# Fetching the first expert's last 128 rows two steps later: attention, a dense layer and eight experts on one core

## The chip, the cores and the metric

The kernel runs on 1 core of one Trainium2 chip. The metric is the device time of one execution in microseconds (us), from the first to the last instruction and what the launch puts around them. TensorE is called PE here, VectorE DVE, ScalarE ACT, GpSimd POOL; SP is the queue that issues most transfers.

## The reference

Three parts follow each other. The first is an attention over 4 batches, 8 heads, 576 positions and 64 features: a coarse one over means of 4 positions plus a local one in a band of 7. Its output is laid out as 2304 tokens of 512 features. The second is a dense layer, the third a mixture of experts in which each token goes to one of 8 experts:

```python
h = x @ w_in; x = (h * np.cos(h)) @ w_out
logits = x @ w_gate
expert_idx = np.argmax(logits, axis=1)
...
for e in range(E):
    mask = expert_idx == e
    xe = x[mask]
    ye = np.maximum(xe @ w1[e], 0.0) @ w2[e]
    out[mask] = gate_w[mask, None] * ye
```

## The kernel before

Products are made in float32 precision: each operand is split into a high part and a rest, and three matmuls (high by high, high by rest, rest by high) are summed. The dense layer runs over 9 blocks of 256 tokens and 8 pairs of hidden chunks (`hidden`, `project`); the attention of the later batches is woven into it. After each block `route` finds each token's expert and scatters its number into lists in DRAM (`lists`), one list per expert and parity.

Before the last block, `freeze` picks the expert with most tokens so far. It is the first expert to run (e = 0 below), and its first 256 rows are known then; its last 128 rows (window 2) and the order of the others are known only when the last block is routed. So the first expert runs in two parts. The loop over f = 0 to 7 in `run` computes windows 0 and 1: `expert_hidden` makes hidden chunk f + 2 (tiles `eph`, then `hh` on ACT and `hl` on DVE) and `expert_project` adds chunk f to the two sums `eacc`. Then `expert_late` makes the hidden layer of window 2 in one piece (`eph_late`, `late`, `latet`), and a second loop projects it.

`expert_fetch` brings an expert's rows. SP loads two rows of token numbers (`listed`), DVE takes the smaller of each pair (L602), PE transposes the result (`ids_ps`, L605), DVE makes indices of it (`esrc`, `ids`, L607 and L609), and POOL gathers the rows (`rows`, L613). `expert_rows` then turns each 128 rows on PE (`ext`, L631), ACT copies them as the high part (`exh`, L633) and DVE subtracts for the rest (`exl`, L634). `expert_chunk` loads a chunk of the next expert's two weights (`raw`, two transfers of 512 KB, L574) and splits each into high part and rest, two casts on ACT (L579) and two subtractions on DVE (L580) for each; `put` scales a sum (`y`, L704) and scatters it to the output.

In the loop over f the calls stand so: at f = 2 the fetch of window 2, at f = 4 the fetch of the next expert's three windows (e = 1), at f = 5 `expert_rows` of window 2, and at odd f one chunk (0 to 3) of the next expert's weights. A block `issue_after` ties the transposition of token numbers on PE behind the last matmul written before it (`self.lastmm`).

The order in which the instructions stand on each engine is not the order of the code. A scheduler decides it when the program is built, from its own estimate of when each operand is ready; on the chip each engine then works through its list in that order and waits where an operand is missing.

Of the kernel before, what the change touches and what calls it, by code (L numbers as in the profile page):

```python
# [32 lines left out]
class Kernel:  # L33
# [556 lines left out]
        nc.vector.reciprocal(gt, sm)  # L590
        return gt

    def expert_fetch(self, e, w0, nw, last, behind=None):

        nc, NT = self.nc, self.NT
        n_ = f"{e}_{w0}"
        listed = self.stage.tile([nw, 3, P], I32, tag="w32", bufs=self.W32, name=f"listed{n_}")
        for t in range(2):
            src = self.lists[t][bass.ds(self.number[e] * NT + w0 * P, nw * P), :]
            nc.sync.dma_start(out=listed[:, t, :], in_=src.rearrange("(w p) c -> w (p c)", p=P))  # L600
        idf = listed[:, 2, :].bitcast(F32)
        nc.vector.tensor_tensor(out=idf, in0=listed[:, 0, :], in1=listed[:, 1, :], op=ALU.min)  # L602
        ps = self.psum([P, nw], f"ids_ps{n_}")
        with self.tc.issue_after(behind) if behind else nullcontext():
            nc.tensor.transpose(ps, idf, self.ident[:nw, :nw])  # L605
        src = self.ep.tile([P, self.NW], I32, tag="esrc", bufs=3, name=f"esrc{n_}")
        nc.vector.tensor_scalar(out=src[:, :nw], in0=ps, scalar1=float(last), scalar2=None, op0=ALU.min)  # L607
        ids = self.ep.tile([P, self.NW], I32, tag="ids", bufs=4, name=f"ids{n_}")
        nc.vector.tensor_copy(ids[:, :nw], ps)  # L609
        got = []  # L610
        for w in range(nw):
            rows = self.ep.tile([P, self.RW], F32, tag="rows", bufs=3, name=f"rows{e}_{w0 + w}")
            nc.gpsimd.indirect_dma_start(out=rows, out_offset=None, in_=self.rows[:last + 1, :],  # L613
                                         in_offset=bass.IndirectOffsetOnAxis(ap=src[:, w:w + 1], axis=0))
            got.append((w0 + w, ids[:, w:w + 1], rows))
        return got
# [144 lines left out]
    def run(self):  # L761
        nc, tc, E, NT, KD = self.nc, self.tc, self.E, self.NT, self.KD
# [171 lines left out]
        for s, (i, fp) in enumerate(slots):  # L934
# [35 lines left out]
            if (i, fp) == (self.NB - 2, 6):  # L970
                assert next(routing, 0) == 0
                self.number = self.freeze()
                got = self.expert_fetch(0, 0, 2, i * self.TB - 1)
# [13 lines left out]
        for f in range(self.NFE):  # L987
            if f + 2 < self.NFE:
                hs.append(self.expert_hidden(0, f + 2, xs, 2 * P))
            if f == 1:  # L990
                gates = self.expert_gates(0, got)
                number, over = self.rest()
                self.number += number
            if f == 2:
                got = self.expert_fetch(0, 2, 1, NT - 1, self.lastmm)
            if f == 5:
                self.expert_rows(0, got, xs)
            if f == 4:
                nxt = self.expert_fetch(1, 0, self.windows(1), NT - 1, self.lastmm)
            if f % 2 == 1:  # L1000
                self.expert_chunk(1, f // 2)
            self.expert_project(0, f, hs[f], ((0, 0), (1, 1)))
# [11 lines left out]
        for e in range(1, E):  # L1014
            gates = self.expert_gates(e, nxt)
            cols, nw = CAPS[e], self.windows(e)
            last = e == E - 1
# [70 lines left out]
```

## Time and profile before

| what | value |
|---|---|
| median of 3 runs | 875.44 us (874.58 to 875.65) |
| the profiled execution's own time | 877.69 us |
| its span, first to last instruction | 875.9 us |
| mean granted clock of PE | 0.979 |
| PE busy | 830.3 us, 95% of the span |
| DVE busy / ACT busy / POOL busy | 61% / 57% / 23% |
| moved by DMA | 95.87 MB, mean 109 GB/s |

The profile is one execution; its own time is 2.25 us above the median. In a timeline a row gives start, length, engine, line, operation, the tile written and the tiles read, how often, and in brackets the idle time of the engine just before with what ended it. The granted clock is a share: 1.00 stands for 2.4 GHz and 0.50 for 1.2 GHz.

### The profile page before, as it was taken

How to read it: one execution, taken by the hardware profiler on the slowest of the kernel's cores; microseconds unless marked ns; L12 is line 12 of the kernel's file. 1: busy time of each engine (PE TensorE's matmuls, PEld its weight loads, DVE VectorE, ACT ScalarE, POOL GpSimd, SP SyncE). 2: the span in 40 equal slices, each digit the busy share in tenths (PEclk: the TensorE clock that was granted, in tenths of full speed). 3: DMA queues.
4: the chain of work that ended last, by engine and by line, in shares of the span. 5: the costliest groups of instructions: out<-in, count | busy, mean ns of one | idle time of the engine just before them, and what ended most of it. 6: DMA issues, size and time to landing. Idle time of an engine off the chain costs nothing.

```text
span 875.9 us, 16801 instructions
## 1 busy us (share of the span) xinstructions
PE 830.3 (95%) x6130; PEld 711.9 (81%) x6130; DVE 537.7 (61%) x1293; ACT 495.4 (57%) x1246; POOL 197.6 (23%) x356
## 2 busy tenths in 40 slices
PE   6889799999999999999999999999899999999995
PEld 4667578778788888788898888898788888888895
DVE  5885799876444485476666657586447654555320
ACT  5466766676766875675644444583366544544321
POOL 5252344442222212313101010100121112012200
PEclk9989899999999999999999999999899999999998
DMA  9931783233252024022010101241748746446110
GB/s 202 290 79 38 295 247 96 71 82 85 59 167 64 14 76 105 13 73 73 15 49 1 49 1 49 73 123 47 192 143 292 243 135 212 148 160 198 58 38 22
DMA packets 112695, 95.87 MB, mean 109 GB/s; under 512 B 65120, under 2 KB 92844, under 8 KB 112604
## 3 DMA queue, kind: packets, MB, share of 16 engines
q1 hardware_dynamic: 108492, 83.96, 32.8%
q0 software_dynamic: 4112, 10.76, 4.1%
q8 instruction: 50, 0.82, 0.4%
q14 instruction: 41, 0.34, 0.1%
HBM read 81.31 MB, written 13.98 MB: 109 GB/s over the span
## 4 chain that ended last, share of the span: by engine, by line
PE 59%; DMA 6%; issue 5%; ACT 5%; DVE 5%; POOL 2%; POOLq 0%; DVEq 0%; ACTq 0%
PE acc L423 16%; PE h L395 15%; PE eacc L671 10%; PE eph L652 9%; DMA lists<-tokens,posi 2%; ACT p L203 1%; DMA raw<-in_moe_w_dram 1%; DMA out_dram<-y,ids 1%; PE o L261 1%; DVE prod L471 1%; PE o L250 1%; PE ext L631 1%; DMA rows<-rows,esrc 1%; PE ptd L238 1%; PE eph_late L689 1%
## 5 line engine op out<-in xcount | busy, mean ns | idle before, releaser
L395 PE MATMUL h<-xh,w 128*128 128x256 f32 x1152 | 230.0, 289 | 0.6 <-ACT xh L322 0.5
L423 PE MATMUL acc<-w,gh 128*128 128x512 f32 x576 | 191.5, 408 | 10.9 <-issue 4.5
L395 PEld LDWEIGHTS h<-xh,w 128*128 128x128 f32 x1152 | 185.8, 192 | 5.5 <-DVE w L366 0.9
L395 PE MATMUL h<-xl,w 128*128 128x256 f32 x576 | 165.4, 287 | 1.4 <-DVE xl L323 1.4
L423 PEld LDWEIGHTS acc<-w,gh 128*128 128x128 f32 x576 | 103.4, 190 | 30.6 <-issue 4.7
L423 PE MATMUL acc<-w,gl 128*128 128x512 f32 x288 | 117.6, 408 | 1.8 <-DVE gl L409 1.8
L652 PE MATMUL eph<-exh,w 128*128 128x256 f32 (+5 forms) x512 | 118.1, 307 | 0.0
L395 PEld LDWEIGHTS h<-xl,w 128*128 128x128 f32 x576 | 110.5, 192 | 4.2 <-DVE xl L323 1.6
L580 DVE TENSOR_TENSOR w<-raw,w 128x512 fp32r<-128x512 f32 x128 | 83.3, 687 | 32.5 <-ACT w L579 32.2
L671 PE MATMUL eacc<-w,hh 128*128 128x512 f32 (+4 forms) x304 | 99.2, 407 | 0.3 <-ACT hh L660 0.3
L652 PEld LDWEIGHTS eph<-exh,w 128*128 128x128 f32 x512 | 87.9, 190 | 3.3
L579 ACT CAST w<-raw 128x512 fp32r<-128x512 f32 x128 | 73.6, 618 | 29.3 <-DMA raw<-in_moe_w_dram 16.3
L401 ACT ACTIVATE u<-h 128x512 int32<-128x512 f32 x72 | 43.2, 600 | 79.7 <-PE h L395 79.6
L652 PE MATMUL eph<-exl,w 128*128 128x256 f32 (+5 forms) x256 | 78.7, 307 | 0.0
L405 DVE SCALAR_TENSOR_TENSOR u<-u,h 128x512 f32<-128x512 f32 x72 | 49.3, 684 | 47.6 <-ACT u L404 47.2
L402 DVE SCALAR_TENSOR_TENSOR u<-h,u 128x512 f32<-128x512 f32 x72 | 49.4, 686 | 38.5 <-ACT u L401 36.3
L471 DVE SCALAR_TENSOR_TENSOR prod<-row,wgb 128x512 f32<-128x512 f32 x96 | 67.1, 699 | 7.4 <-ACT row L465 6.0
L423 PEld LDWEIGHTS acc<-w,gl 128*128 128x128 f32 x288 | 54.5, 189 | 14.4 <-DVE gl L409 2.5
L408 ACT CAST gh<-u 128x512 fp32r<-128x512 f32 x72 | 44.6, 619 | 35.8 <-DVE u L405 21.3
L499 POOL DMA_INDIRECT lists<-tokens,posi x18 | 19.0, 1057 | 198.2 <-DVE posi L496 192.3
L403 ACT ACTIVATE u<-u 128x512 f32<-128x512 f32 x72 | 45.5, 632 | 31.8 <-DVE u L402 30.8
L671 PEld LDWEIGHTS eacc<-w,hh 128*128 128x128 f32 (+4 forms) x304 | 52.1, 182 | 12.0 <-ACT hh L660 0.8
(177 smaller groups left out, 1416.3 us busy)
## 6 DMA issues: line engine op xcount, KB each, us to landing
raw<-in_moe_w_dram SPq DMA_DIRECT2D x64, 512.0 KB
f<-in_moe_w_in_dram SPq DMA_DIRECT2D x8, 1024.0 KB
f<-in_moe_w_out_dram SPq DMA_DIRECT2D x8, 1024.0 KB
rows<-row SPq DMA_DIRECT2D x9, 520.0 KB
xraw<-xT SPq DMA_DIRECT2D x14, 256.0 KB
rawk<-in_k_dram SPq DMA_DIRECT2D x48, 72.0 KB
rawv<-in_v_dram SPq DMA_DIRECT2D x24, 144.0 KB
rawq<-in_q_dram SPq DMA_DIRECT2D x32, 80.0 KB
```

The costliest lines, as they stand in the source:

```text
L395: nc.tensor.matmul(ph[:, fo, :], lhsT=a[:, kk, f], rhs=b[:, kk, :], start=(n == 0), stop=(n == 3 * self.KD - 1))
L401: nc.scalar.activation(turns, hv, AF.Copy, scale=1.0 / (2 * math.pi))
L402: nc.vector.scalar_tensor_tensor(out=u, in0=hv, scalar=1.0 / (2 * math.pi), in1=turns, op0=ALU.mult, op1=ALU.subtract)
L403: nc.scalar.activation(u, u, AF.Sin, scale=PI)
L405: nc.vector.scalar_tensor_tensor(out=u, in0=u, scalar=1.0, in1=hv, op0=ALU.subtract, op1=ALU.mult, reverse0=True)
L408: nc.scalar.copy(gh, u)
L423: nc.tensor.matmul(self.acc[i][t], lhsT=a[:, fo, t * P:(t + 1) * P], rhs=b[:, fo, :], start=(f == 0 and n == 0), stop=(f == self.NF - 1 an ...
L471: nc.vector.scalar_tensor_tensor(out=prod, in0=row[:, t, :DM], scalar=1.0, in1=self.spread[e // 2][:, e % 2, :], op0=ALU.mult, op1=ALU.mul ...
L579: nc.scalar.copy(hi, raw[:, sl])
L580: nc.vector.tensor_tensor(out=lo, in0=raw[:, sl], in1=hi.bitcast(F32), op=ALU.subtract)
L652: self.lastmm = nc.tensor.matmul(ph, lhsT=a[:, kk, f % 2 * P:(f % 2 + 1) * P], rhs=b[:, kk, :cols], start=(n == 0), stop=(n == 3 * self.KD ...
L671: self.lastmm = nc.tensor.matmul(self.eacc[w][:m], lhsT=a[:, at * P:at * P + m], rhs=b[:, f % 2, :], start=(f == 0 and n == 0), stop=(f == ...
```

## The change

`expert_fetch` is cut in two. `expert_list` holds its first half (the two transfers of token numbers and the minimum on DVE) and is still called at f = 2 for window 2; the second half (transposition, indices, gather) now follows at f = 4. The turning of window 2's rows goes from f = 5 to f = 7, and the whole fetch of the next expert from f = 4 to f = 6.

```diff
-    def expert_fetch(self, e, w0, nw, last, behind=None):
+    def expert_list(self, e, w0, nw):
...
         idf = listed[:, 2, :].bitcast(F32)
         nc.vector.tensor_tensor(out=idf, in0=listed[:, 0, :], in1=listed[:, 1, :], op=ALU.min)
+        return idf
+
+    def expert_fetch(self, e, w0, nw, last, behind=None, idf=None):
+
+        nc = self.nc
+        n_ = f"{e}_{w0}"
+        if idf is None:
+            idf = self.expert_list(e, w0, nw)
         ps = self.psum([P, nw], f"ids_ps{n_}")
...
             if f == 2:
-                got = self.expert_fetch(0, 2, 1, NT - 1, self.lastmm)
-            if f == 5:
+                idf = self.expert_list(0, 2, 1)
+            if f == 4:
+                got = self.expert_fetch(0, 2, 1, NT - 1, self.lastmm, idf)
+            if f == 7:
                 self.expert_rows(0, got, xs)
-            if f == 4:
+            if f == 6:
                 nxt = self.expert_fetch(1, 0, self.windows(1), NT - 1, self.lastmm)
```

The lists below show what the scheduler makes of both. In a name the first number is the step f (of `eph`, `hh`, `hl`), the window (of `ids_ps`, `ext`, `rows`, `y`, `eacc`) or the chunk (of `raw`), the last a serial number; lines of the changed kernel are 8 higher.

On PE, the transposition of window 2's token numbers (`ids_ps_2`) in the loop of the first expert, before:

```order
L671 MATMUL eacc_1_7813<-w_1_7544,hl_4_7986 128x512
L652 MATMUL eph_7_8083<-exh_7389,w_0_7602 128x256
L605 MATMUL ids_ps_2_7993<-ident,listed_2_7989 128x1
L652 MATMUL eph_7_8083<-exl_7390,w_0_7602 128x256
L652 MATMUL eph_7_8083<-exh_7389,w_0_7602 128x256 x2
```

and now:

```order
L679 MATMUL eacc_1_7813<-w_1_7544,hl_4_7986 128x512
L660 MATMUL eph_7_8067<-exh_7389,w_0_7602 128x256
L613 MATMUL ids_ps_2_8053<-ident,listed_2_7989 128x1
L660 MATMUL eph_7_8067<-exl_7390,w_0_7602 128x256
L660 MATMUL eph_7_8067<-exh_7389,w_0_7602 128x256 x2
```

It stands between the same two matmuls as before. Nothing ahead of it on PE has moved either.

On PE, the end of that loop and the start of `expert_late`, before (`ids_ps_0` is the next expert's transposition, `ext_2` the turning of window 2's rows):

```order
L671 MATMUL eacc_1_7813<-w_1_7609,hl_6_8058 128x512
L671 MATMUL eacc_0_7812<-w_1_7609,hh_7_8096 128x512
L605 MATMUL ids_ps_0_8065<-ident,listed_0_8061 128x3
L631 MATMUL ext_2_8100<-ident,rows_2_7999 128x128 x4
L671 MATMUL eacc_0_7812<-w_1_7609,hh_7_8096 128x512
L671 MATMUL eacc_0_7812<-w_1_7609,hl_7_8097 128x512
L671 MATMUL eacc_1_7813<-w_1_7609,hh_7_8096 128x512 x2
L671 MATMUL eacc_1_7813<-w_1_7609,hl_7_8097 128x512
L689 MATMUL eph_late_8167<-w_0_7407,exh_7389 128x256
L689 MATMUL eph_late_8193<-w_0_7537,exh_7389 128x256
L689 MATMUL eph_late_8167<-w_0_7407,exl_7390 128x256
```

and now:

```order
L679 MATMUL eacc_1_7813<-w_1_7609,hl_6_8050 128x512
L679 MATMUL eacc_0_7812<-w_1_7609,hh_7_8080 128x512 x2
L679 MATMUL eacc_0_7812<-w_1_7609,hl_7_8081 128x512
L679 MATMUL eacc_1_7813<-w_1_7609,hh_7_8080 128x512 x2
L679 MATMUL eacc_1_7813<-w_1_7609,hl_7_8081 128x512
L613 MATMUL ids_ps_0_8108<-ident,listed_0_8104 128x3
L639 MATMUL ext_2_8126<-ident,rows_2_8059 128x128 x4
L697 MATMUL eph_late_8167<-w_0_7407,exh_7389 128x256
L697 MATMUL eph_late_8193<-w_0_7537,exh_7389 128x256
L697 MATMUL eph_late_8167<-w_0_7407,exl_7390 128x256
```

The two went behind five matmuls of the loop and stand now right ahead of the matmuls that read `exh` and `exl`.

DVE and ACT in the same stretch. DVE before:

```order
L602 TENSOR_TENSOR listed_0_8061<-listed_0_8061 3x128
L661 SCALAR_TENSOR_TENSOR hl_7_8097<-eph_7_8083,hh_7_8096 128x256
L607 TENSOR_SCALAR esrc_0_8067<-ids_ps_0_8065 128x3
L609 CAST ids_0_8069<-ids_ps_0_8065 128x3
L589 TENSOR_SCALAR esm_2_8234<-esm_2_8234 128x1
L590 RECIPROCAL gt_2_8236<-esm_2_8234 128x1
L634 TENSOR_TENSOR exl_7390<-ext_2_8100,exh_7389 128x4x128
L580 TENSOR_TENSOR w_0_8109<-raw_2_0_8107,w_0_8109 128x512 x2
```

DVE now:

```order
L669 SCALAR_TENSOR_TENSOR hl_7_8081<-eph_7_8067,hh_7_8080 128x256
L589 TENSOR_SCALAR esm_2_8234<-esm_2_8234 128x1
L590 RECIPROCAL gt_2_8236<-esm_2_8234 128x1
L580 TENSOR_TENSOR w_0_8086<-raw_2_0_8084,w_0_8086 128x512 x2
L580 TENSOR_TENSOR w_1_8093<-raw_2_1_8091,w_1_8093 128x512 x2
L602 TENSOR_TENSOR listed_0_8104<-listed_0_8104 3x128
L615 TENSOR_SCALAR esrc_0_8110<-ids_ps_0_8108 128x3
L617 CAST ids_0_8112<-ids_ps_0_8108 128x3
L580 TENSOR_TENSOR w_0_8135<-raw_3_0_8133,w_0_8135 128x512 x2
L642 TENSOR_TENSOR exl_7390<-ext_2_8126,exh_7389 128x4x128
```

ACT before:

```order
L587 ACTIVATE ex_2_8233,esm_2_8234<-rows_2_7999 128x8
L633 CAST exh_7389<-ext_2_8100 128x4x128
L579 CAST w_0_8109<-raw_2_0_8107 128x512 x2
L579 CAST w_1_8116<-raw_2_1_8114 128x512 x2
L704 ACTIVATE y_0_8153<-eacc_0_7812,gt_0_7857 128x512
L579 CAST w_0_8135<-raw_3_0_8133 128x512 x2
```

ACT now:

```order
L587 ACTIVATE ex_2_8233,esm_2_8234<-rows_2_8059 128x8
L579 CAST w_0_8086<-raw_2_0_8084 128x512 x2
L579 CAST w_1_8093<-raw_2_1_8091 128x512 x2
L712 ACTIVATE y_0_8153<-eacc_0_7812,gt_0_7857 128x512
L712 ACTIVATE y_1_8158<-eacc_1_7813,gt_1_7863 128x512
L579 CAST w_0_8135<-raw_3_0_8133 128x512 x2
L641 CAST exh_7389<-ext_2_8126 128x4x128
```

On DVE the minimum of the next expert's token numbers went behind the four subtractions of weight chunk 2, and `exl` behind two of chunk 3; on ACT `exh` went behind four casts of chunk 2, both `y` and two casts of chunk 3. On SP the next expert's token numbers are now loaded after chunk 2 and not before it, and on POOL the scatter of `y_0` stands ahead of the next expert's three gathers and not behind them.

## Rows read from the trace of the kernel before

**Rows 1.** The page's part 1: busy time, share and instructions of PE.
```profile
PE 830.3 (95%) x6130; PEld 711.9 (81%) x6130; DVE 537.7 (61%) x1293; ACT 495.4 (57%) x1246; POOL 197.6 (23%) x356
```

**Rows 2.** Windows: length, busy PE, PEld, DVE, ACT, POOL, clock, DMA share, GB/s.
```profile
653.00:866.00 213.00, 212.41 (x1196) 185.69 (x1195) 103.51 (x218) 99.76 (x219) 35.89 (x35) 1.00 0.49 159
```

**Rows 3.** Timeline of PE, the end of the first expert's loop.
```profile
629.07 0.23 PE L605 MATMUL ids_ps<-ident,listed 1*128 1x1 f32 x1 [4.04 <-DVE listed L602]
...
631.75 1.05 PE L671 MATMUL eacc<-w,hh 128*128 128x512 f32 x2
...
633.03 1.05 PE L671 MATMUL eacc<-w,hh 128*128 128x512 f32 x2
...
635.36 0.63 PE L671 MATMUL eacc<-w,hh 128*128 128x512 f32 x2
...
636.07 0.39 PE L671 MATMUL eacc<-w,hh 128*128 128x512 f32 x1
636.39 0.22 PE L605 MATMUL ids_ps<-ident,listed 3*128 3x3 f32 x1
636.54 0.66 PE L631 MATMUL ext<-ident,rows 128*128 128x128 f32 x4
636.96 0.48 PE L671 MATMUL eacc<-w,hh 128*128 128x512 f32 x1
...
638.20 0.40 PE L689 MATMUL eph_late<-w,exh 128*128 128x256 f32 x2
638.60 0.39 PE L689 MATMUL eph_late<-w,exl 128*128 128x256 f32 x1
```

**Rows 4.** Timeline of ACT, the same stretch.
```profile
629.46 1.14 ACT L579 CAST w<-raw 128x512 fp32r<-128x512 f32 x2 [0.21 <-DMA raw<-in_moe_w_dram]
...
635.93 0.19 ACT L587 ACTIVATION_READ_ACCUMULATOR ex<-rows 128x1 f32 x1
637.24 0.59 ACT L633 CAST exh<-ext 128x512 fp32r<-128x512 f32 x1 [1.12 <-PE ext L631]
637.72 2.18 ACT L579 CAST w<-raw 128x512 fp32r<-128x512 f32 x4
639.80 0.69 ACT L704 ACTIVATE y<-eacc,gt 128x512 f32<-128x512 f32 x1
640.38 1.14 ACT L579 CAST w<-raw 128x512 fp32r<-128x512 f32 x2
...
644.00 0.21 ACT L587 ACTIVATE ex<-rows 128x8 f32<-128x8 f32 x1
```

**Rows 5.** Timeline of DVE, the same stretch.
```profile
628.65 0.27 DVE L602 TENSOR_TENSOR listed<-listed 1x128 f32<-1x128 int32 x1
...
636.65 0.16 DVE L607 TENSOR_SCALAR esrc<-ids_ps 128x3 int32<-128x3 f32 x1 [1.61 <-PE ids_ps L605]
...
637.86 0.69 DVE L634 TENSOR_TENSOR exl<-ext,exh 128x512 fp32r<-128x512 f32 x1 [0.72 <-ACT exh L633]
638.46 3.86 DVE L580 TENSOR_TENSOR w<-raw,w 128x512 fp32r<-128x512 f32 x6
```

**Rows 6.** Timeline of the SP queue: transfers of the next expert's weights.
```profile
623.86 1.00 SPq L574 DMA_DIRECT2D raw<-in_moe_w_dram  x2
...
628.76 0.39 SPq L574 DMA_DIRECT2D raw<-in_moe_w_dram  x1
```

**Rows 7.** Timeline of POOL: the last gather of the next expert's rows.
```profile
640.27 0.95 POOL L613 DMA_INDIRECT rows<-rows,esrc  x1 [0.30 <-ACT w L579]
```

**Rows 8.** Timeline of PE: another wait, in the dense layer.
```profile
351.71 0.81 PE L215 MATMUL sd<-kd,qdbd 128*128 128x144 f32 x2 [1.84 <-POOL qdbd L184]
```

**Rows 9.** Windows as in rows 2, around three waits of PE.
```profile
351.00:356.00 5.00, 4.29 (x23) 4.29 (x24) 1.06 (x6) 1.63 (x10) 2.78 (x8) 0.66 0.02 5
628.00:636.00 8.00, 6.93 (x24) 6.07 (x25) 4.50 (x12) 4.17 (x9) 0.98 (x1) 0.57 0.89 259
237.00:240.00 3.00, 1.60 (x15) 1.36 (x14) 1.62 (x6) 1.64 (x5) 1.13 (x3) 1.00 0.02 0
```

## Prediction

> **What bounds the kernel now.** I read the page first: PE is busy for 95% of the span [rows 1], so the kernel ends when PE has gone through its list, and a change counts by the PE time that it adds or removes. Next came the windows behind the place of the change: from 653 us to 866 us PE is busy 212.41 of 213.00 us [rows 2]. There is no slack there that could take up a delay; what PE loses at 640 us arrives whole at the end. Then the timelines of PE, ACT and DVE over the end of the first expert's loop. On PE they show one long wait, 4.04 us ahead of the transposition of window 2's token numbers [rows 3]. It is ended by DVE's minimum at L602, which starts at 628.65 us behind subtractions of weights [rows 5], and the clock is low afterwards: 0.57 in the mean from 628 to 636 us [rows 9].
>
> **What the change does not do.** Its words aim at that wait: if the transposition stood two steps later, PE would have matmuls to do instead of waiting. But the order of instructions has it between the same two matmuls of `eph` 7 before and after, and the minimum that ends the wait keeps its place on DVE. The old call at f = 2 was already put as late as that by the scheduler. So I cost this part at nothing: 0 us, up to about 629 us the two kernels are one.
>
> **What it moves.** Three things go later. The next expert's transposition and the turning of window 2's rows stood in the middle of the last step on PE, and the last five matmuls of that step followed them. Those matmuls were the cover under which ACT made `exh` and DVE `exl`: the turning starts at 636.54, `exh` at 637.24, `exl` at 637.86, and the `eph_late` matmuls that read them go on at 638.20 and 638.60 with no wait to speak of [rows 3 to 5]. Now that cover is spent beforehand, and what remains is worked through in a row.
>
> PE, end of the step: a group of three matmuls takes 635.36 to 636.07 = 0.71 us, 0.235 each [rows 3]. The six of step 7 start at 636.07 and the last starts 5 x 0.235 later, ending 0.39 after that: 637.64. There PE wants the transposition.
>
> The transposition waits for the minimum on DVE, which now stands behind the four subtractions of chunk 2. ACT is free at 635.93 + 0.19 = 636.12 and can cast chunk 2 at once; one cast is 0.62 (four in 2.18, so one every 0.52) [rows 4]. DVE starts at 636.12 + 0.62 + about 0.06 = 636.80; six subtractions take 3.86, one every 0.634 [rows 5], so the instruction after the fourth starts at 636.80 + 4 x 0.634 = 639.34. From the start of the minimum to the transposition were 628.65 to 629.07 = 0.42 us [rows 3, 5]: PE goes on at 639.76, after 2.1 us of waiting. The turning follows 0.15 later (636.39 to 636.54), at 639.91, and ends at 640.57.
>
> `exh` may start 0.70 after the turning's start (636.54 to 637.24): 640.61. Is ACT free? Four casts of chunk 2 until the first `y` took 637.72 to 639.80 = 2.08, a `y` 0.58 until the next (639.80 to 640.38) [rows 4]: 636.12 + 2.08 + 2 x 0.58 + 2 x 0.52 = 640.40. It is, so moving the two `y` and the casts ahead costs nothing by itself, with 0.2 us to spare.
>
> `exl` may start 0.62 after `exh`: 641.23. But DVE has two subtractions of chunk 3 ahead of it. The indices start 0.26 after the transposition (636.39 to 636.65), take some 0.15 for both, and 640.17 + 2 x 0.634 = 641.44. The first `eph_late` matmul on `exl` came 0.74 after `exl`'s start (637.86 to 638.60): 642.18 in place of 638.60 [rows 3, 5]. **First term: 642.18 - 638.60 = 3.6 us.** Its lower bound is the same chain with DVE free (641.23 + 0.74 - 638.60 = 3.4); without the row of waits being exact I allow 3.0. From there on the same matmuls follow as before.
>
> **The clock.** In those 4.5 us PE works for about 1.2 us. The trace of before has waits with and without a fall of the clock. The wait of 1.84 us at 351.71 [rows 8] had one: the mean from 351 to 356 us is 0.66 [rows 9], that is (1 - 0.66) x 2 x 5 = 3.4 us at 0.50, 1.2 GHz, with PE at work for nearly all of it. From 237 to 240 us, with PE busy 1.60 of 3 us, the clock stayed at 1.00 [rows 9]. The new stretch is emptier than both, so I take one fall as long as the first. What a low clock costs: a group of three matmuls took 631.75 to 633.03 = 1.28 us there against 0.71 [rows 3], 45% of the time lost. **Second term: 3.4 x 0.45 = 1.5 us.** Below it is 0; above it the longer fall, (1 - 0.57) x 2 x 8 = 6.9 us from 628 to 636 [rows 9], at most 6.9 x 0.45 = 3.1 us. The Trainium skill, in "TensorE: Matmul & The Clock Gate" under Terms, puts the penalty at the slow time x (1 - K/N), half of it at 1.2 GHz. By that the second term would be 1.7 and the sum 5.3; the rows have 0.45, and the sum goes by them.
>
> **Edits at nothing, and their cover.** The next expert's token numbers are loaded on SP after chunk 2. The pair of transfers begun at 623.86 was awaited last at 629.46, 5.6 us later [rows 4, 6], under full traffic; by that the numbers, issued just after chunk 2's second transfer at 628.76 [rows 6], are there by 635, and DVE wants them at 639.3. The same 5.6 has chunk 2 there by 634.4, ahead of 636.12, so ACT's earlier casts don't wait. If that cover failed, each us late would be a us on PE. The next expert's gathers on POOL come behind the scatter of `y_0`: y ends near 638.9, then three issues of 0.95 + 0.30 before the last gather [rows 7], about 642.8. The last gather of before was issued at 640.27 and its rows were read at 644.00, at most 3.7 us later [rows 4, 7]: 646.5. ACT reads them now ahead of `late`, whose matmuls with 3.6 us of delay still run then. Nothing, or 0.2 us.
>
> **The sum.** 3.6 + 1.5 = 5.1 us. The profiled execution's own 877.69 would be 882.8, its span 875.9 would be 881.0. That execution lies 2.25 us above the median of the runs, 875.44; on the median the prediction is **880.5 us**.
>
> **The rivals.**
> - *The clock holds.* The 1.60 of 3 us stretch speaks for it, the emptier new stretch and the 1.84 us wait against. Then 875.4 + 3.6 = 879.0. Chance 0.20.
> - *The clock stays low for longer*, as after 628 us. 875.4 + 3.6 + 3.1 = 882.1. Chance 0.13.
> - *The new waits are hidden*: for it, DVE and ACT have idle time over the whole span (61% and 57% busy [rows 1]); against, PE's next matmuls read `exh` and `exl` themselves, and nothing else is on its list. 875.4. Chance 0.07.
> - *Faster: the transposition of window 2 does move on the chip* and PE's wait at 625 to 629 us goes. It decides by whether matmuls stand between `eph` 7's first matmul and the transposition. The price is at most the 4.04 us of idle and the low clock behind it, 3.1 us: 875.4 - 7.1 = 868.3. Against it stands the order, where no matmul has come between. Chance 0.04.
> - The forecast, both terms: 0.56.
>
> **How the numbers follow.** The likeliest case gives 880.5. The range takes in the case without a clock loss with the first term at 3.0 (878.4), and the longer fall with a little on top for `late` and the runs' own scatter (882.1 + 0.5 = 882.6); it leaves out the hidden and the faster case and some tails, together 2 in 10. A measurement of this kernel tells 0.2% (1.75 us) from no change: slower by more than that are the first two rivals and the forecast, less a little, 0.87; within it 0.08; faster 0.05.
>
> **What would show it.** In the profile of the changed kernel: the same 4 us wait at L613 near 629 us; a second wait of about 2 us ahead of the next transposition, with DVE's minimum as its end; then 0.6 to 0.7 us ahead of the first `eph_late` matmul, ended by `exh`, and about 0.5 us ahead of the third, ended by `exl`; the granted clock at 0.50 for some 3 us behind; from there the old sequence, 5 us later. The prediction is wrong if the first wait is gone, if the minimum at L602 comes before the subtractions of chunk 2, or if PE finds idle time after 653 us that it did not have.

## The result and the profile after

The change made the kernel slower: **884.16 us** in the median of four executions (881.5 to 892.32) against 875.01 (873.69 to 875.65) of the kernel before on the same chip, ratio 1.0112, 95% interval 1.008 to 1.0143. That is 9.15 us, where 5.1 were forecast; the time lies 1.6 us above the range. Timed twice more with the kernel before beside it, the same change came out at 1.0078 (1.0043 to 1.0114; 886.36 against 880.49) and 1.0063 (1.003 to 1.0096; 886.15 against 880.75): 5.9 and 5.4 us. So two things have to be explained: the 5 to 6 us that come back each time, and the rest of the first 9.15.

The profiled execution took 881.5 us, its span is 879.7. Part 1 of its page, the busy times, against [rows 1]:

```profile
PE 832.0 (95%) x6130; PEld 712.8 (81%) x6130; DVE 537.6 (61%) x1293; ACT 494.7 (56%) x1246; POOL 197.5 (22%) x356
```

The number of instructions is unchanged on every engine. Now PE's timeline over the end of the first expert's loop, against [rows 3] (the new lines of code push the numbers down by 8: L605 is L613, L689 is L697):

```profile
626.86 0.23 PE L613 MATMUL ids_ps<-ident,listed 1*128 1x1 f32 x1 [3.48 <-DVE listed L602]
...
633.75 0.40 PE L679 MATMUL eacc<-w,hl 128*128 128x512 f32 x1
636.48 0.22 PE L613 MATMUL ids_ps<-ident,listed 3*128 3x3 f32 x1 [2.34 <-DVE listed L602]
636.63 0.92 PE L639 MATMUL ext<-ident,rows 128*128 128x128 f32 x4
638.23 0.80 PE L697 MATMUL eph_late<-w,exh 128*128 128x256 f32 x2 [0.68 <-ACT exh L641]
638.95 0.58 PE L697 MATMUL eph_late<-w,exl 128*128 128x256 f32 x1
639.33 0.63 PE L697 MATMUL eph_late<-w,exh 128*128 128x256 f32 x2
...
639.97 0.63 PE L697 MATMUL eph_late<-w,exh 128*128 128x256 f32 x2
...
644.01 0.40 PE L697 MATMUL eph_late<-w,exh 128*128 128x256 f32 x2
...
644.37 0.40 PE L697 MATMUL eph_late<-w,exh 128*128 128x256 f32 x2
```

The old wait is still there (3.48 in place of 4.04). Behind the last matmul of step 7 (633.75) PE now waits 2.34 us for DVE's minimum, then 0.68 for ACT's `exh`. A group of three `eph_late` matmuls then takes 0.64 us (639.33 to 639.97), and from 644.01 on 0.36, as before the change. DVE and ACT over the same stretch, against [rows 4, 5]:

```profile
633.72 2.50 DVE L580 TENSOR_TENSOR w<-raw,w 128x512 fp32r<-128x512 f32 x4 [0.16 <-ACT w L579]
636.14 0.28 DVE L602 TENSOR_TENSOR listed<-listed 3x128 f32<-3x128 int32 x1
...
636.95 1.29 DVE L580 TENSOR_TENSOR w<-raw,w 128x512 fp32r<-128x512 f32 x2
638.21 0.69 DVE L642 TENSOR_TENSOR exl<-ext,exh 128x512 fp32r<-128x512 f32 x1
```

```profile
633.09 2.16 ACT L579 CAST w<-raw 128x512 fp32r<-128x512 f32 x4
635.15 1.25 ACT L712 ACTIVATE y<-eacc,gt 128x512 f32<-128x512 f32 x2
...
637.59 0.58 ACT L641 CAST exh<-ext 128x512 fp32r<-128x512 f32 x1 [0.16 <-PE ext L639]
```

The minimum stands behind four subtractions of chunk 2, and `exl` behind two of chunk 3. The windows behind (columns as in [rows 2], the clock is the third number from the end), after and then before:

```profile
636.00:640.00 4.00, 2.85 (x12) 2.21 (x13) 3.68 (x9) 3.05 (x6) 3.05 (x3) 0.61 0.34 105
640.00:644.00 4.00, 4.00 (x21) 4.00 (x21) 0.45 (x3) 0.30 (x2) 1.97 (x2) 0.54 0.71 225
644.00:655.00 11.00, 10.75 (x67) 8.85 (x66) 4.09 (x9) 4.50 (x11) 0.00 (x0) 1.00 0.01 3
```

```profile
636.00:640.00 4.00, 4.00 (x25) 3.19 (x25) 2.60 (x8) 2.88 (x8) 2.07 (x2) 1.00 0.48 156
640.00:644.00 4.00, 4.00 (x36) 4.00 (x35) 3.64 (x7) 4.00 (x11) 2.06 (x2) 1.00 0.70 227
```

The clock, at 1.00 throughout before, falls to 0.50 for a part of both windows.

**A ruler that does not move.** Up to the first expert's loop all kernels here run the same instructions, yet they get there at different times. So positions are counted from the first `eacc` matmul of that loop (610.33 us in the profile after, 611.98 before). Each number below is one start in a kernel's PE timeline less that; the last is the span less that.

| kernel | loop begins at | window 2's transposition | first `eph_late` on `exl` | first `latet` | end of span |
|---|---|---|---|---|---|
| before | 611.98 | 17.09 | 26.62 | 32.24 | 263.92 |
| before_again | 623.44 | 16.95 | 25.48 | 31.10 | 263.66 |
| after | 610.33 | 16.53 | 28.62 | 36.32 | 269.37 |
| after_again | 616.84 | 17.33 | 29.95 | 37.72 | 269.16 |
| after_third | 612.95 | 17.58 | 30.35 | 37.46 | 268.85 |
| next_fetch_back | 625.30 | 17.77 | 27.43 | 33.05 | 266.30 |
| next_fetch_only | 614.04 | 17.63 | 26.71 | 32.57 | 265.56 |
| turn_behind_step | 615.32 | 18.08 | 28.67 | 34.29 | 266.88 |
| filled_wait | 613.55 | 17.37 | 30.23 | 36.33 | 267.55 |
| later_window_2 | 616.68 | 17.51 | 28.57 | 35.25 | 266.82 |
| numbers_before_weights | 612.75 | 16.27 | 25.21 | 30.85 | 263.25 |
| casts_behind_relu | 614.41 | 16.47 | 25.94 | 34.23 | 266.49 |
| later_with_indices_first | 612.39 | 17.83 | 26.10 | 33.21 | 266.11 |
| after_step_7_relu | 612.79 | 17.20 | 27.56 | 33.18 | 265.01 |

From the loop to the end, the change takes 268.85 to 269.37 us in three executions and the kernel before 263.66 to 263.92 in two: **5.3 us** between the means. That is the change. The ruler has a grain too. The two profiles of the kernel before differ by 1.14 us at the first `latet` (32.24 and 31.10), though by only 0.26 at the end, and from `latet` to the end the kernels of the table take anything from 231.2 to 233.3 us. So a difference of 1 to 2 us between two single profiles is not told by it; the means at `latet`, 37.17 against 31.67, give 5.5 for the change. The beginning of the loop scatters from 610.33 to 616.84 us, and is at 623 and 625 in two executions that ran slow at the start (last section).

### The profile page after: what moved, and what is told of

Same layout as the page of the kernel before. It is cut to its first block, busy times and chain, and to the rows that moved or that the text cites. A ratio compares the mean times of both kernels' runs of the same rounds, so it can differ in the third digit from the quotient of the medians.

```text
span 879.7 us, 16802 instructions
## 1 busy us (share of the span) xinstructions
PE 832.0 (95%) x6130; PEld 712.8 (81%) x6130; DVE 537.6 (61%) x1293; ACT 494.7 (56%) x1246; POOL 197.5 (22%) x356
## 4 chain that ended last, share of the span: by engine, by line
PE 60%; DMA 7%; issue 6%; ACT 4%; DVE 3%; POOL 2%; SPq 0%; POOLq 0%; DVEq 0%; ACTq 0%
PE acc L423 18%; PE h L395 17%; PE eacc L679 9%; PE eph L660 8%; DMA raw<-in_moe_w_dram 2%; DMA rows<-rows,esrc 1%; PE o L261 1%; DMA out_dram<-y,ids 1%; PE o L250 1%; DMA rows<-row 1%; PE eph_late L697 1%; ACT p L203 1%; PE ext L639 1%; PE s L199 1%; DMA lists<-tokens,posi 1%
## 5 line engine op out<-in xcount | busy, mean ns | idle before, releaser
L713 POOL DMA_INDIRECT out_dram<-y,ids x22 | 22.1, 1003 | 186.6 <-ACT y L712 168.1
```

## The experiments

**The change and the kernel before, unaltered.** Edit: none.

> The changed kernel unaltered, for a second trace and more times. Theory A (the two new waits ahead of the late layer, 2.3 + 0.7 us, and the low clock behind them are all of the loss): ratio 1.005 to 1.007 (879.5 to 881 us), and the new trace shows the same two waits and no others. Theory B (beside these a later stage, the loading of the third expert's weights from 655 to 692 us, loses time too, differently in each execution): ratio 1.009 to 1.013, and the new trace has PE waits of 1 us or more in all between 655 and 720 us that the kernel before does not have.

> The kernel before unaltered, for a second trace. One wait of 3.5 to 4.1 us ahead of the transposition of window 2's token numbers, no other wait of PE over 0.5 us after 600 us. Under theory B the stage from 655 to 692 us shows as little waiting as in the first trace; if it shows 1 us or more here too, the scatter belongs to both kernels and B says nothing of the change.

Measured: the ratio 1.0078 above. The waits of the change came back:

```profile
634.17 0.19 PE L613 MATMUL ids_ps<-ident,listed 1*128 1x1 f32 x1 [4.30 <-DVE listed L602]
...
644.37 0.22 PE L613 MATMUL ids_ps<-ident,listed 3*128 3x3 f32 x1 [2.78 <-DVE listed L602]
...
646.02 0.79 PE L697 MATMUL eph_late<-w,exh 128*128 128x256 f32 x2 [0.68 <-ACT exh L641]
```

Behind 650 us this execution has no wait of PE over 0.4 us. The first profile after did have some: PE was busy 209.47 of 211.00 us from 655 to 866, with two waits of 0.54 and 0.57 for `hh`. The kernel before and its variants show such waits in some executions too (0.56 us in next_fetch_only), so theory B, a loss of the change in that stage, falls. In the first profile that stage did take longer: 233.05 us from `latet` to the end, against 231.44 and 231.39 in the other two. before_again has its one long wait (3.90 us) and no other over 0.4 behind it, as expected; its one execution took 888.85 us.

> The change unaltered once more. If the 9 us of the first comparison were the change's, the ratio comes out near 1.011 again; if 5.5 us are the change's and the rest is a difference between executions that starts ahead of the changed code, 1.006 to 1.008, and in the profile the time from the first eacc matmul of the first expert to the end of the span is 269.2 to 269.4 us against 263.7 to 263.9 of the kernel before.

Measured: ratio 1.0063, 268.85 us from the loop to the end, 0.35 less than expected. The reading that 5.5 us are the change's holds; that of 9 falls.

**One half of the change each.** Edit of the first: the change with `if f == 4` in place of `if f == 6` at the next expert's fetch. Edit of the second, in the kernel before:

```diff
-            if f == 4:
+            if f == 6:
                 nxt = self.expert_fetch(1, 0, self.windows(1), NT - 1, self.lastmm)
```

> The change without its last part: the next expert's fetch goes back from step 6 to step 4, all else as changed. On PE the next expert's transposition and the turning of window 2 stand again in the middle of the last step. Theory A and B: the two new waits vanish, the time is that of the kernel before within 0.3% (875 us). If instead the late turning of window 2 at step 7 were the cause, it would stay at 881 us or more.

> The kernel before with one part of the change alone: the next expert's fetch at step 6 in place of 4. The turning of window 2 then stands a step earlier, and the next expert's transposition inside the late layer, so no wait ahead of the late layer: theory A gives the time of before within 0.3% (873 to 877 us). If a late gather of the next expert's rows is what costs (a rival, C), PE waits for these rows behind the late layer and the time rises by 2 us or more.

Measured: next_fetch_back 1.0011 (0.9985 to 1.0036), no second wait, no clock fall behind step 7 (`exl` to `latet` 5.62 us as before):

```profile
650.12 0.22 PE L613 MATMUL ids_ps<-ident,listed 3*128 3x3 f32 x1
...
652.73 0.38 PE L697 MATMUL eph_late<-w,exl 128*128 128x256 f32 x1 [0.40 <-DVE exl L642]
```

So by its time what the change says of window 2 costs nothing that can be told, and the moved fetch of the next expert is needed for the loss. (Its one profile ends 2.4 to 2.6 us later on the ruler than the kernel before, 0.8 to 2.0 of it by `latet`; the ratio does not bear that out.) But alone the moved fetch does not make the whole loss: next_fetch_only 1.0034 (1.0011 to 1.0056), some 3 us. There the scheduler put the late transposition among the `eph_late` matmuls, with work all around, and the turning stayed covered:

```profile
643.25 0.22 PE L605 MATMUL ids_ps<-ident,listed 3*128 3x3 f32 x1
```

The time is just outside theory A's 0.3%, and rival C's wait is not there either: PE waits 0.78 us for `latel` and 0.56 for `hh` behind the late layer, and nowhere for the gathered rows. What the 3 us are is not shown. The two waits of the change came only with both of its halves: with the turning at f = 7 as well, everything that waits stands in one row at the end of the step.

**The late minimum and the lost cover apart.** Edit: the change, with the next expert's numbers listed at f = 4, and its transposition and the turning tied behind the last matmul of step 7.

```diff
             if f == 4:
+                idn = self.expert_list(1, 0, self.windows(1))
...
             self.expert_project(0, f, hs[f], ((0, 0), (1, 1)))
+            if f == 7:
+                nxt = self.expert_fetch(1, 0, self.windows(1), NT - 1, self.lastmm, idn)
+                self.expert_rows(0, got, xs)
```

> The next expert's token numbers are listed where the kernel before lists them (ahead of chunk 2, on SP and on DVE), but their transposition and the turning of window 2's rows are tied behind the last matmul of step 7 on PE, as the change has them. So the late minimum on DVE is taken out of the change, the lost cover stays. Theory A (the change costs a late minimum, 2.3 us, plus a lost cover, plus the clock): no wait ahead of the transposition; the turning begins at the end of the step, which was 25.66 us behind the first eacc matmul of the first expert, plus 0.15, and from the turning's start to the first eph_late matmul on exl it takes 2.06 as before: 27.9 us from the first eacc matmul in place of 26.6 (before) and 28.6 to 30.0 (change). So 1.3 us, and 0 to 1.5 for the clock: ratio to the kernel before 1.0015 to 1.003. Rival D (the place at the end of the step costs all, the minimum nothing): as the change, ratio 1.006 to 1.011.

Measured: 1.0015 (0.9983 to 1.0047). PE's timeline:

```profile
641.30 0.40 PE L679 MATMUL eacc<-w,hl 128*128 128x512 f32 x1
641.63 0.22 PE L613 MATMUL ids_ps<-ident,listed 3*128 3x3 f32 x1
641.78 0.66 PE L639 MATMUL ext<-ident,rows 128*128 128x128 f32 x4
643.11 0.50 PE L697 MATMUL eph_late<-w,exh 128*128 128x256 f32 x2 [0.68 <-ACT exh L641]
643.99 0.39 PE L697 MATMUL eph_late<-w,exl 128*128 128x256 f32 x1 [0.37 <-DVE exl L642]
```

```profile
641.00:645.00 4.00, 2.96 (x18) 2.08 (x18) 3.11 (x7) 3.00 (x6) 1.86 (x2) 1.00 0.18 48
```

No wait ahead of the transposition, 0.68 and 0.37 behind the turning, and the clock stays at 1.00. From the last matmul of step 7 to the first `eph_late` on `exl` it takes 2.69 us; in the kernel before it took 638.60 - 637.97 = 0.63, and 0.57 for transposition and turning, which stood ahead (636.39 to 636.96 in [rows 3]), so 1.20:

```profile
637.97 0.39 PE L671 MATMUL eacc<-w,hl 128*128 128x512 f32 x1
```

The lost cover costs 1.5 us. In the change the same stretch takes 5.20, 5.60 and 4.63 us: 4.0, 4.4 and 3.4 over 1.20. The late minimum, with the transfers that this edit also puts ahead of chunk 2 on SP, makes the difference, 1.9 to 2.9 us, and rival D falls. The first `eph_late` on `exl` comes at 28.67 us on the ruler where 27.9 were expected; the first wait, which is no part of the edit, is 5.04 us here in place of 4.04.

**The clock apart.** Edit: the change with PE kept at work while it waits. The 18 transpositions are extra and their result is not used; the next expert's transposition and the turning are tied behind them (shown in part).

```diff
+                spare = self.psum([P, 4, P], "spare")
+                with self.tc.issue_after(self.lastmm):
+                    for k in range(18):
+                        self.lastmm = nc.tensor.transpose(spare[:, k % 4, :], self.ident, self.ident).ins
```

> The change with its order unaltered, and 18 transpositions of the identity into a spare PSUM tile that nothing reads, put on PE between the last matmul of step 7 and the next expert's transposition: at 0.105 us each (four of ext from 636.54 to 636.96 us before) 1.9 us of work in the place of the wait for the late minimum. The minimum is as late as in the change, so the first term stays; only what PE does meanwhile differs. Theory A (a second term of 1.5 to 2.1 us is the clock, which falls after the idle stretch): the granted clock stays at 1.00 behind, the first matmul of eph_late on exl to the first latet takes 5.62 us as before in place of 7.1 to 7.8, and the end comes 1.5 to 2.1 us earlier than with the change, counted from the first eacc matmul of the first expert (267.1 to 267.6 us in place of 268.9 to 269.4); ratio to the kernel before 1.003 to 1.005. Rival H (the slow eph_late has another cause, such as late operands or the DMA traffic): 7.1 to 7.8 us as in the change, ratio 1.006 to 1.008.

Measured: 1.0031 (1.0005 to 1.0058), 267.55 us from the loop to the end.

```profile
639.38 2.12 PE L1015 MATMUL spare<-ident 128*128 128x128 f32 x18
641.44 0.22 PE L613 MATMUL ids_ps<-ident,listed 3*128 3x3 f32 x1
641.59 0.66 PE L639 MATMUL ext<-ident,rows 128*128 128x128 f32 x4
642.92 0.50 PE L697 MATMUL eph_late<-w,exh 128*128 128x256 f32 x2 [0.68 <-ACT exh L641]
643.78 0.39 PE L697 MATMUL eph_late<-w,exl 128*128 128x256 f32 x1 [0.36 <-DVE exl L642]
```

```profile
640.00:644.00 4.00, 2.97 (x22) 2.34 (x21) 3.53 (x9) 3.85 (x8) 2.48 (x3) 1.00 0.17 66
644.00:650.00 6.00, 5.67 (x47) 5.47 (x47) 1.88 (x8) 1.56 (x8) 3.14 (x3) 1.00 0.62 181
```

The operands come no earlier (from step 7's last matmul to `exl` 4.63 us, as in after_third), but the clock holds, and `exl` to `latet` is 6.10 us (0.33 of it a wait for `late`) in place of the change's 7.11 to 7.77; 5.62 had been expected. The end comes 1.3 to 1.8 us earlier than in the change. So the second term is the clock, and rival H falls.

**Can the first wait be had?** It is the larger one, and in both kernels. Edit of the first try, in the change: window 2's fetch at f = 6, both lists where the kernel before has them.

```diff
-            if f == 4:
+            if f == 6:
                 got = self.expert_fetch(0, 2, 1, NT - 1, self.lastmm, idf)
...
+            if f == 4:
+                idn = self.expert_list(1, 0, self.windows(1))
             if f == 6:
-                nxt = self.expert_fetch(1, 0, self.windows(1), NT - 1, self.lastmm)
+                nxt = self.expert_fetch(1, 0, self.windows(1), NT - 1, self.lastmm, idn)
```

> Here the transposition of window 2's token numbers really moves on PE: behind the four matmuls of eacc of step 5, since the step's instructions are put behind the last matmul of f = 6; both lists stay where the kernel before has them. Theory A: the minimum at L602 still starts at its old time, so the first wait falls from 4 us to about 1.5 at most (11 matmuls of eph and 4 groups of eacc stand ahead of it now, about 2.4 us at full clock); but the gather of the rows starts no earlier and the turning stands at the end of step 7: it waits for the rows, about 0.95 + 3.7 us behind the indices less 2.8 us of matmuls, some 2 us, and the lost cover costs 1.3: no gain, ratio 0.997 to 1.004. Rival F (the wait of 4 us is simply covered): ratio 0.993 to 0.995.

Measured: 1.007 (1.0038 to 1.0102), slower than expected by either theory.

```profile
631.84 0.74 PE L679 MATMUL eacc<-w,hh 128*128 128x512 f32 x2 [0.80 <-ACT hh L668]
...
634.19 0.19 PE L613 MATMUL ids_ps<-ident,listed 1*128 1x1 f32 x1 [0.28 <-DVE listed L602]
...
642.77 1.08 PE L639 MATMUL ext<-ident,rows 128*128 128x128 f32 x4 [4.15 <-DMA rows<-rows,esrc]
```

The wait of 4 us is covered, as the change's words promise (0.28 us are left, and 0.80 for `hh` ahead of it), and it comes back whole at the turning: 4.15 us for the rows, and a low clock behind (`exl` to `latet` 6.68 us).

**Is it DVE's order?** Edit: the calls at the steps of the kernel before or one earlier, with chunk 0's casts and subtractions written behind window 2's fetch, the subtractions tied behind its index operations; chunk 1's behind step 4. The part at f = 2:

```diff
+                got = self.expert_fetch(0, 2, 1, NT - 1, self.lastmm, idf)
+                with self.tc.issue_after(self.lastid):
+                    for which in range(2):
+                        self.cast_w(1, 0, which, raws[which])
```

> A version meant to beat both: the token numbers of window 2 are loaded as before, behind chunk 0's weights on SP, but the four subtractions of chunk 0 are tied on DVE behind the minimum and the two index operations, and chunk 1's casts are written behind step 4. The minimum can start once its transfers have landed (issued at 622.93 us before, landed perhaps at 625.5) in place of 628.65. Theory A (the first wait of 4 us is DVE's, not the transfer's): the wait falls to 1 to 1.5 us, the low clock behind it shortens, the gather starts 3 us earlier; some of it may return as a wait ahead of the next expert's transposition, whose minimum stands behind subtractions of chunk 1: ratio 0.993 to 0.998. Rival G (the transfer of the numbers lands only shortly before 628 us): the wait stays at 3 to 4 us, ratio 0.999 to 1.003.

Measured: 0.9977 (0.9954 to 1.0), at the edge of what can be told and in theory A's range; but the wait that theory A wanted shorter is 4.05 us, so the 2 us, if they are real, are not from it. DVE's timeline:

```profile
628.26 0.42 DVE L678 SCALAR_TENSOR_TENSOR hl<-eph,hh 128x256 fp32r<-128x256 f32 x1 [7.56 <-ACT hh L677]
628.61 0.27 DVE L611 TENSOR_TENSOR listed<-listed 1x128 f32<-1x128 int32 x1
```

The subtractions are gone from in front of the minimum; now `hl` of step 5 stands there, behind ACT's `hh`, and that behind casts whose weights had not landed. The next edit took those away too, by writing chunk 0's casts at f = 4, tied behind `hh` of step 6, and chunk 1's at f = 5. Against the run just shown:

```diff
-                with self.tc.issue_after(self.lastid):
+                with self.tc.issue_after(self.lasthh), self.tc.issue_after(self.lastid):
```

> The version before this one left the first wait at 4.05 us, since DVE's minimum stood behind hl of step 5, that behind ACT's hh of step 5, and that behind ACT's first two casts of chunk 0, which waited 6.57 us for their transfer. Here ACT's casts of chunk 0 are tied behind hh of step 6, so that hh and hl of steps 5 and 6 and the minimum no longer stand behind that transfer; chunk 1's casts come behind step 5. Theory A' (the first wait is the in-order queue of ACT that waits for weights nobody needs yet): the minimum starts when its own transfers have landed, about 625.5 to 626.5 us on the time scale of the kernel before, the wait falls from 4 us to 1 to 2, the clock falls for less or not at all, and the later waits of the loop (hh of step 7 behind chunk 1's transfer, the next expert's minimum) take back 1 to 2 us: ratio 0.994 to 0.998. Rival G (the token numbers themselves land as late as 628): wait of 3.5 to 4 us, ratio 0.998 to 1.002.

Measured: 1.0022 (0.9992 to 1.0051), wait 4.26 us. It went as rival G had it:

```profile
630.46 0.28 DVE L611 TENSOR_TENSOR listed<-listed 1x128 f32<-1x128 int32 x1 [5.28 <-DMA listed<-lists]
```

```profile
626.68 0.73 SPq L609 DMA_DIRECT2D listed<-lists  x2
```

DVE stands idle and waits for the token numbers themselves: two transfers of 0.5 KB, issued at 626.68, used at 630.46, 3.8 us later, with 1 MB of weights under way. With none of the orders tried does the minimum come much before 16 us behind the start of the loop (16.67 before, 15.86 and 16.05 in these two). One more link stands ahead of the transfers: before it issues them SP waits for a scatter into `lists` to land, 4.1 us here and 2.7 in the kernel before. POOL issued the last of these scatters at 619.88, 6.8 us ahead of the transfers. So it is not shown that the numbers can't come sooner: no run scattered earlier, or held chunk 0's weights back behind the numbers. And chunk 0's later casts hold up the weights behind them: `latet` waits 2.52 us.

**Cover it, and hurry what follows.** Edits: later_window_2 with chunk 1's casts written behind the fetch, its subtractions tied behind the index operations, and chunk 2 loaded at f = 6; and the same with the fetch at f = 5.

> The run with window 2's transposition behind step 5 covered the first wait (0.28 us left, and 0.80 for hh of step 5), and lost it again at the turning, 4.15 us for the rows: their gather was issued 3.3 us behind the transposition, since DVE's index operations stood behind four subtractions of chunk 1. Here chunk 1's casts and subtractions are written behind the fetch and tied on DVE behind the two index operations. Theory A'' (the first wait is for the transfer of the token numbers, which no order can hurry, so it can only be covered; what follows must then not be late): gather about 1 us behind the transposition, rows 5.1 us later (as measured there), so the turning waits 1.5 to 2 us in place of 4.15, exh and exl 1.0 more; against the kernel before the first eph_late on exl comes 0.5 to 2 us earlier: ratio 0.996 to 1.0. Rival J (the rows are late because the queue is full of weights, whatever the order): the turning waits 3.5 us or more, ratio 1.002 to 1.006.

> As the other kernel of this pair, but window 2's transposition stands behind the last matmul of eph 7, not behind eacc of step 5: 10 matmuls of 256 columns, 1.2 us, cover a part of the first wait, and the turning stands inside step 7 again, so that exh and exl are covered. Theory A'': first wait 2.5 to 3 us in place of 4.0 to 4.3; a wait for the rows of 0 to 2.5 us ahead of the turning; no waits for exh and exl: ratio 0.996 to 1.001. Rival J: rows 3.5 us or more late, ratio 1.001 to 1.004.

Measured: 1.0031 (1.0001 to 1.0061) and 1.004 (1.0005 to 1.0076), neither as expected. In the first the gather went out 0.7 us behind the transposition, not 3.5, and the turning still waited, between what the two theories had:

```profile
636.44 0.66 PE L648 MATMUL ext<-ident,rows 128*128 128x128 f32 x4 [2.69 <-DMA rows<-rows,esrc]
...
647.46 0.66 PE L712 MATMUL latet<-ident,late 128*128 128x128 f32 x4 [1.26 <-ACT late L708]
```

In the second PE waited 2.85 us at the transposition, as expected, not at all for the rows, and 1.18 and 0.63 ahead of the matmuls on `exh` and `exl`, where no wait had been expected. Its first `exl` matmul comes at 27.56 us, no earlier than before. No version beat the kernel before clearly.

## Why the prediction was off

By its steps:

- **The first wait stays.** Right: 3.48, 4.30 and 4.54 us in three executions of the change. That the words of the change aim at it and the order does not was the reading that decided the sign. The rival in which it goes was tried in later_window_2: the wait goes, and comes back as a wait for the rows.
- **First term, 3.6 us.** Measured 4.0, 4.4 and 3.4. Its chain was right link by link: minimum behind four subtractions of chunk 2, 2.34 us (1.81 to 2.78) against 2.1, then 0.68 us for `exh` (0.6 to 0.7 expected). On the ruler the first `eph_late` on `exl` comes at 29.64 in the mean of three against 26.05 of two: 3.6. Of the 0.5 for `exl`, 0.43 shows in one execution; in the other two the matmuls ahead ran at half clock until it was there.
- **Second term, 1.5 us.** `exl` to `latet` took 7.70, 7.77 and 7.11 us in place of 5.62: 2.1, 2.1 and 1.5. The price per us was right: three matmuls 0.64 in place of 0.36 us, 44% lost. Only the low stretch was longer than 3.4 us: a share of 0.61 and 0.54 over 2 x 4 us is (0.39 + 0.46) x 8 = 6.8 us. That is as long as the row of 6.9 us that was kept as the upper end. Some 4.7 us of it, from 638.95 to 643.7 where the matmuls take up their full pace, lie in this stretch, and 4.7 x 0.44 = 2.1. The new stretch was emptier than the one it was sized by.
- **The price of the low clock against the Trainium skill.** At 0.50, 1.2 GHz, a matmul of 256 columns follows the one before it after 0.213 us (0.64 / 3). At 1.00 it follows after 0.12 (0.36 / 3). The Trainium skill, "TensorE: Matmul & The Clock Gate", section "Back-to-back issue gap", has formulas for matmuls in isolation (N / 1.2 and N / 2.4 + 2.5 ns for N columns) that give 0.213 and 0.109 us as estimates for 256 columns; the first agrees, the second is lower than the rows, and this is why the rows lose 44% and not the half that the Trainium skill has under Terms.
- **Edits at nothing.** Right. The rows of the next expert came late for ACT (waits of 1.92 and 2.92 us for `ex`), but the first `late` at 645.22 still ended ahead of PE's need, and `latet` waited 0.2 us as before.
- **PE idle behind 653 us** that it did not have was to count against the prediction. The first profile has 0.9 us of it (1.53 idle in 211 us against 0.59 in 213 [rows 2]); the other two have no wait over 0.4 us there, so it is not the change's.
- **The step that failed** is in how the numbers follow: the sum was put on the median of three runs within 1.1 us of each other, and the range got 0.5 us for `late` and the runs' own scatter. That term was mis-sized: executions of the change spread over 10.8 us in the first comparison alone (881.5 to 892.32). The sum itself, 5.1 us, measured 5.3 on the fixed ruler, and 5.4 and 5.9 in the two later comparisons. The kernel before had medians of 875.01, 880.4 to 880.75 and 882.66 us on its several occasions, and the loop begins anywhere from 610.33 to 616.84 us in kernels with the same instructions up to there. The first profiled execution of the change took 881.5 us, inside the range, with the loop 1.65 us earlier than in the profile before; the untraced ones took 883.45 to 892.32. Where these lost their time no trace shows. That the excess over 5 us lay ahead of the loop is argued from the others, not shown.

So the mechanism held, the direction too. Of the sizes the first term held and the second came out 0.4 us low (3.6 and 1.9 on the ruler up to `latet`); that the sum meets the 5.3 at the end within 0.2 us is partly luck, since two profiles of one kernel differ by 1.1 us on the ruler at `latet`. The range was wrong because it took three agreeing runs for the spread of all.

## What to carry to other kernels

Look where an edit puts the instructions on each engine, not what its words say: this one left the wait that it named in place and took away the cover of another. Work that is waited for in a chain (transpose, copy, subtract) belongs among matmuls that do not need it; each link put behind them is paid in full, and the clock may be paid on top (it was in the change, and was not in turn_behind_step). Before a wait is moved, ask which of its causes is last: here several orders stood in front of the minimum, and behind them all a small transfer that waits for a scatter to land and that no order tried here hurried. And compare two kernels from a point up to which they are the same; the median of the kernel before moved by up to 7.65 us between occasions (875.01 to 882.66), more than the effect.

## What had not been expected of the hardware

- **A low clock under full work.** In before_again PE was busy 20.00 of 20 us from 20 to 40 us and was granted 0.50 all that time; in the kernel before the same stretch has 0.91. It cost some 10 us (the first `h` matmul behind it starts at 43.67 in place of 32.42, and the loop begins at 623.44 in place of 611.98), and next_fetch_back has it too (19.93 busy, 0.51). Up to 37 us the matmuls there all have `ident` as an operand; ahead of them PE had waited 1.12 and 2.06 us for `rawv` in these two, 0.73 in the kernel before. What decided it is not shown. The rows of before_again and of before:

```profile
20.00:40.00 20.00, 20.00 (x71) 9.32 (x71) 8.34 (x22) 6.94 (x24) 5.92 (x13) 0.50 0.85 289
```

```profile
20.00:40.00 20.00, 18.15 (x170) 13.43 (x169) 15.70 (x37) 8.88 (x30) 6.56 (x15) 0.91 0.99 307
```

- **The same wait with and without a fall.** The 1.84 us at 351.71 [rows 8] left 0.66 behind it; 1.86 us at the same place in the profile after, with the same instructions ahead at the same times, left 1.00:

```profile
351.74 0.51 PE L215 MATMUL sd<-kd,qdbd 128*128 128x144 f32 x2 [1.86 <-POOL qdbd L184]
```

```profile
351.00:356.00 5.00, 4.26 (x36) 4.25 (x37) 1.26 (x7) 2.22 (x11) 2.76 (x8) 1.00 0.03 7
```

So a single wait of such a length decides nothing about the clock, and a price for it has to keep both ends.
